# Retention followed by a SoLU feed-forward: chunk 3 loaded before w_out, w_out scaled mostly on GpSimd, key-value products moved next to the values, and new orders for the first chunks and the end

## The chip, the cores and the metric

The kernel runs on one core of a Trainium2 chip. The metric is the device time of one execution in microseconds (us). The kernel before takes 239.58 us, the median of 3 runs (239.53 to 240.38). One core has a matrix engine (TensorE, "PE" in the profile, with its weight loads as "PEld"), a vector engine (DVE), an activation engine (ACT), GpSimd (POOL) and a queue engine (SP) that here issues nearly all DMAs.

## The reference

Retention (causal attention with a decay per head and no softmax) over batch 8, heads 8, sequence 576, head size 64, and behind it a two-layer block with a SoLU activation and a layer norm, over all 4608 tokens:

```python
scores = q @ k.T / sqrt(64)                       # per batch and head
ret    = scores * where(i >= j, gamma[h] ** (i - j), 0)
x      = (ret @ v), heads side by side            # (4608, 512)
h      = x @ w_in                                 # (4608, 1024)
e      = exp(h - max(h))
solu   = h * e / sum(e)
ln     = (solu - mean(solu)) / sqrt(var(solu) + 1e-6) * g_ln
out    = ln @ w_out                               # (4608, 512)
```

All inputs and the output are float32; the kernel multiplies in float16.

## The kernel before

The tokens are cut into 36 chunks of 128 rows. Batches go in pairs: for one pair, chunks alternate between the two batches (four chunks of 128 positions each), and a ninth chunk takes the last 64 positions of both; that one is called a tail here. So chunks 8, 17, 26 and 35 are tails. Retention is computed in its chunked form: within a chunk by masked scores, and across chunks by a running state for each batch.

One chunk n goes through these helpers:

- `ld` (L111): three loads, q, k and v, of 256 KB each from SP's queue (six of half the size for a tail). Six chunks fit in the load pool.
- `cast` (L123): on GpSimd, q and v times the decay (two-input multiplies, L131 and L138), k cast to float16 (L137). For chunks 0 to 2 (`first`), q goes to DVE and k to ACT.
- `transpose_qk`, `evict_qk` (L149, L157): eight transposes on PE, and a copy out of PSUM by DVE or ACT.
- `scores`, `mask` (L168, L181): eight matmuls that use 64 rows of the array, and two masked copies on DVE.
- `state`, `state_update` (L192, L205, L208, L216): the key-value product `kp`, eight matmuls that write 64 columns of the array; DVE adds the old state, GpSimd decays it. Tails have neither.
- `values`, `evict_x` (L230, L236, L246): eight matmuls of 64 columns (masked scores times v), then four full-size ones (state times q), and a copy by ACT.
- `mm1`, `row_max`, `exps`, `solu` (L254, L263, L269, L279): x times w_in in eight matmuls of 512 columns; row maximum on DVE; exp on ACT; h times exp on DVE, with its sum.
- `spread` (L294 to L302): sum of squares on ACT, and three tiny GpSimd instructions that make the row scale `rs`.
- `transpose_u`, `evict_u` (L309, L314): eight transposes and a copy (ACT).
- `mm2`, `store` (L321, L328, L331): u times w_out in eight matmuls of 512 columns; ACT multiplies by `rs` on the way out; one DMA (two for a tail).

Before `mm2` can run for the first time, w_out is prepared once: `load_w_out` (four DMAs of 512 KB), `scale_w_out` (w_out times g_ln, cast to float16: eight ACT instructions, one for each block of 128 rows, L347), `mean_w_out` (L354, the column means by eight matmuls with a matrix of ones) and `centre_w_out` (L363, eight DVE instructions that write w_out anew with the means taken off, so that the layer norm's mean need not be taken from u).

The schedule is written by hand: each engine runs its instructions in the order of the program text, and an instruction waits for semaphores only. After a prologue (chunks 0 and 1 up to x, chunk 0 up to its exp), a loop over i runs from 1 to 36. Its turn i works on several chunks at once: transposes, scores, state and values of chunk i+1, the cast of chunk i+2, `mm1` of chunk i, `solu`, `spread` and `transpose_u` of chunk i-1, `evict_u` of chunk i-2, and `mm2` and `store` of chunk i-3 (LAG). In a turn, PE's order is: tp(i+1), h(i), sc(i+1), kp(i+1), o(i-3), x(i+1), lp(i-1), by the names of the tiles that are written. Turns 1 and 2 have another order (`early`): `mm1` and `row_max` come first, and the preparation of w_out stands in turn 2. The loads are issued in the order: chunks 0, 1, w_in, chunk 2, w_out, chunks 3, 4, 5; then one chunk in each turn. PSUM has four banks of a common tag `ps` (tp, sc, kp, o, x, lp, mean take turns in them) and two pairs of banks for h.

Of the kernel before, what the change touches and what calls it, by code (L numbers as in the profile page):

```python
# [10 lines left out]
FP = mybir.dt.float32  # L11
F16 = mybir.dt.float16
P = 128
H = 8
D = 64
LAG = 3
# [27 lines left out]
def kernel(  # L44
# [10 lines left out]
    nc = tc.nc  # L55
    B, _, S, _ = q.shape
    NTOK, DM = out.shape
    DFF = moe_w_in.shape[1]
    NF = DFF // P
    ACT = mybir.ActivationFunctionType  # L60
    ALU = mybir.AluOpType
# [23 lines left out]
    def rows(n):  # L85

        bs, c = chunks[n]
        if c < 4:
            return [(slice(0, P), bs[0], c * P)]
        return [(slice(64 * i, 64 * i + 64), b, 4 * P) for i, b in enumerate(bs)]  # L90
# [20 lines left out]
    def ld(n):  # L111
        qf = load.tile([P, H, D], FP, name="qf")
        kf = load.tile([P, H, D], FP, name="kf")
        vf = load.tile([P, H, D], FP, name="vf")
        for src, dst in ((q, qf), (k, kf), (v, vf)):
            for pp, b, s0 in rows(n):
                m = pp.stop - pp.start
                nc.sync.dma_start(  # L118
                    out=dst[pp], in_=src[b, :, s0 : s0 + m, :].rearrange("h p d -> p h d")
                )  # L120
        T["ld", n] = qf, kf, vf
# [32 lines left out]
    def evict_qk(n, copy=None):  # L154
        tp = T.pop(("tp", n))
        qkT = att.tile([P, 2, 4, P], F16, name="qkT")
        (copy or nc.vector.tensor_copy)(  # L157
            out=qkT.rearrange("p a b c -> p (a b c)"), in_=tp.rearrange("p a b c -> p (a b c)")
        )
        T["qkT", n] = qkT  # L160
# [88 lines left out]
    def mm1(n, by_rows=False):  # L249
        xT = T.pop(("xT", n))  # L250
        h = ps_h.tile([P, DFF], FP, name="h")
        order = [(i, dc) for i in range(2) for dc in range(4)]
        for i, dc in sorted(order, key=lambda o: o[1]) if by_rows else order:
            nc.tensor.matmul(  # L254
                out=h[:, i * 512 : (i + 1) * 512], lhsT=xT[:, dc],
                rhs=w_in16[:, dc, i * 512 : (i + 1) * 512],
                start=dc == 0, stop=dc == 3,
            )
        T["hps", n] = h

    def row_max(n):
        nm = tiny.tile([P, 1], FP, name="nm")
        nc.vector.tensor_reduce(out=nm, in_=T["hps", n], axis=AX.X, op=ALU.max, negate=True)  # L263
        T["nm", n] = nm

    def exps(n):
        e = moe.tile([P, DFF], FP, name="e")
        s = tiny.tile([P, 1], FP, name="s")
        nc.scalar.activation(  # L269
            out=e, in_=T["hps", n], func=ACT.Exp, bias=T.pop(("nm", n)), accum_out=s  # L270
        )
        T["e", n] = e, s

    def solu(n):
        e, s = T["e", n]
        u = moe.tile([P, DFF], F16, name="u")
        su = tiny.tile([P, 1], FP, name="su")
        nmu = tiny.tile([P, 1], FP, name="nmu")
        nc.vector.scalar_tensor_tensor(  # L279
            out=u, in0=T.pop(("hps", n)), scalar=1.0, in1=e, op0=ALU.mult, op1=ALU.mult,  # L280
            accum_out=su,
        )
        nc.vector.tensor_scalar(  # L283
            out=nmu, in0=su, scalar1=-1.0 / DFF, scalar2=None, op0=ALU.mult, op1=ALU.bypass
        )
        T["u", n] = u, nmu
# [16 lines left out]
        T["rs", n] = rs  # L303

    def transpose_u(n):
        u, _ = T.pop(("u", n))
        lp = ps.tile([P, NF, P], F16, tag="ps", name="lp")
        for c in range(NF):
            nc.tensor.transpose(out=lp[:, c], in_=u[:, c * P : (c + 1) * P], identity=ident)  # L309
        T["lp", n] = lp  # L310
# [3 lines left out]
        (copy or nc.scalar.copy)(out=uT, in_=T.pop(("lp", n)))  # L314
        T["uT", n] = uT

    def mm2(n):
        uT = T.pop(("uT", n))
        o = ps.tile([P, DM], FP, tag="ps", name="o")
        for c in range(NF):  # L320
            nc.tensor.matmul(  # L321
                out=o, lhsT=uT[:, c], rhs=w_out16[:, c], start=c == 0, stop=c == NF - 1
            )
        T["o", n] = o

    def store(n):
        o_sb = moe.tile([P, DM], FP, name="o_sb")
        nc.scalar.activation(out=o_sb, in_=T.pop(("o", n)), func=ACT.Copy, scale=T.pop(("rs", n)))  # L328
        for pp, b, s0 in rows(n):
            m = pp.stop - pp.start  # L330
            nc.sync.dma_start(out=out[b * S + s0 : b * S + s0 + m, :], in_=o_sb[pp])  # L331

    def load_w_in(a):
        nc.sync.dma_start(out=w_in32[:, a], in_=moe_w_in[a * P : (a + 1) * P, :])  # L334
# [7 lines left out]
        w = moe_w_out.rearrange("(c p) m -> p c m", p=P)  # L342
        nc.sync.dma_start(out=w_out32[:, 2 * i : 2 * i + 2], in_=w[:, 2 * i : 2 * i + 2])  # L343

    def scale_w_out(cs):
        for c in cs:
            nc.scalar.activation(  # L347
                out=w_out16[:, c], in_=w_out32[:, c], func=ACT.Copy, scale=g32[:, c : c + 1]
            )

    def mean_w_out():
        mean = ps.tile([P, DM], FP, tag="ps", name="mean")
        for c in range(NF):
            nc.tensor.matmul(  # L354
                out=mean, lhsT=ones, rhs=w_out16[:, c], start=c == 0, stop=c == NF - 1
            )
        T["mean"] = mean
# [10 lines left out]
    def on(j):  # L368
        return 0 <= j < NCH

    with tc.manual_schedule():
        nc.sync.dma_start(out=small, in_=nc.inline_tensor(small_np, name="small_c").ap())
        ld(0)
        nc.scalar.dma_start(out=ident, in_=nc.inline_tensor(id_np, name="ident_c").ap())
        nc.scalar.dma_start(
            out=tris.rearrange("p a b -> p (a b)"), in_=nc.inline_tensor(tris_np, name="tris_c").ap()
        )
        nc.scalar.dma_start(out=gln, in_=moe_g_ln.rearrange("(c p) -> p c", p=P))
        ld(1)
        for a in range(4):  # L380
            load_w_in(a)
        ld(2)
        for i in range(4):
            load_w_out(i)
        ld(3)
        ld(4)
        ld(5)
        nc.vector.memset(ones, 1.0 / DFF)
        nc.vector.memset(mhalf, -0.5)


        cast(0, True)
        nc.gpsimd.tensor_scalar(
            out=g32, in0=gln, scalar1=32.0, scalar2=None, op0=ALU.mult, op1=ALU.bypass
        )
        transpose_qk(0)
        evict_qk(0)
        scores(0)
        state(0)
        cast(1, True)  # L400
        transpose_qk(1)
        mask(0)
        state_update(0)
        values(0)
        evict_x(0)
        evict_qk(1)
        scores(1)
        state(1)
        mask(1)
        cast_w_in(0)  # L410
        cast_w_in(1)
        values(1)
        evict_x(1)
        cast_w_in(2)
        cast_w_in(3)
        state_update(1)
        mm1(0, True)
        row_max(0)
        cast(2, True)
        exps(0)  # L420

        for i in range(1, NCH + 1):
            if on(i + 5):
                ld(i + 5)
            early = i < 3
            if early:
                mm1(i)
                row_max(i)  # L430
            if i == 1:
                solu(0)
            if i == 2:
                solu(1)
                scale_w_out(range(NF))
                exps(2)
                mean_w_out()
            if on(i + 1):
                transpose_qk(i + 1)
                evict_qk(i + 1, nc.scalar.copy if i < 5 else None)  # L440
            if i == 1:
                exps(1)
            if on(i + 2):
                cast(i + 2)
            if not early:
                if on(i - 1):
                    solu(i - 1)
                if on(i):
                    mm1(i)
            if on(i - 2):  # L450
                evict_u(i - 2)
            if on(i + 1):
                scores(i + 1)
                mask(i + 1)
                if chunks[i + 1][1] < 4:
                    state(i + 1)
            if on(i - 1):
                spread(i - 1)
            if not early and on(i):
                row_max(i)  # L460
            if on(i + 1) and chunks[i + 1][1] < 4:
                state_update(i + 1)
            if i == 2:
                centre_w_out()
            if on(i - LAG):
                mm2(i - LAG)
                store(i - LAG)
            if i == NCH:
                for j in range(NCH - LAG + 1, NCH - 1):
                    mm2(j)  # L470
                    store(j)
            if on(i + 1):
                values(i + 1)
                evict_x(i + 1)
            if on(i - 1):
                transpose_u(i - 1)
            if not early and on(i):
                exps(i)
        evict_u(NCH - 1, nc.vector.tensor_copy)
        mm2(NCH - 1)  # L480
        store(NCH - 1)


# [28 lines left out]
```

## Time and profile before

| what | value |
|---|---|
| median of the runs | 239.58 us (239.53 to 240.38) |
| the profiled execution | 239.56 us, of which the span from first to last instruction is 237.8 us |
| mean granted TensorE clock | 0.992 |
| PE in the chain that ended last | 74% of the span |
| SP's queue in that chain | 12% |
| costliest PE groups | h (L254) 71.4 us, o (L321) 68.4 us |
| first matmul of h(4), the first turn of the loop's regular order that comes after w_out is ready | 44.42 us |
| first matmul of h(35), the last chunk | 221.30 us |

The span is what the profile's rows cover; 1.76 us of the execution lie around it. "Chain" is the chain of waits followed back from the last instruction. A group's row names the line, the engine, the tile written and the tiles read; chunk numbers in brackets are added here by counting, since the trace leaves buffer numbers out.

### The profile page before, as it was taken

How to read it: one execution, taken by the hardware profiler on the slowest of the kernel's cores; microseconds unless marked ns; L12 is line 12 of the kernel's file. 1: busy time of each engine (PE TensorE's matmuls, PEld its weight loads, DVE VectorE, ACT ScalarE, POOL GpSimd, SP SyncE). 2: the span in 40 equal slices, each digit the busy share in tenths (PEclk: the TensorE clock that was granted, in tenths of full speed). 3: DMA queues.
4: the chain of work that ended last, by engine and by line, in shares of the span. 5: the costliest groups of instructions: out<-in, count | busy, mean ns of one | idle time of the engine just before them, and what ended most of it. 6: DMA issues, size and time to landing. Idle time of an engine off the chain costs nothing.

```text
span 237.8 us, 5729 instructions
## 1 busy us (share of the span) xinstructions
PE 213.9 (90%) x2120; PEld 116.6 (49%) x2120; DVE 174.7 (73%) x294; ACT 172.7 (73%) x271; POOL 172.8 (73%) x275
## 2 busy tenths in 40 slices
PE   0586867899999999999999999999999999999971
PEld 0343334555555555555555555555555555555530
DVE  0537279878888888887788888888878888888530
ACT  2257994977787777777877777777777777777871
POOL 0275189898868899888869999998868999983220
PEclk9999799999999999999999999999999999999999
DMA  7999999998979694898788877978878876111123
GB/s 128 245 351 296 252 225 220 178 242 205 251 176 209 159 215 95 210 235 178 181 182 196 187 166 161 229 188 183 201 175 190 188 139 152 47 45 47 44 90 86
DMA packets 120923, 42.50 MB, mean 179 GB/s; under 512 B 114624, under 2 KB 114752, under 8 KB 120896
## 3 DMA queue, kind: packets, MB, share of 16 engines
q1 hardware_dynamic: 119568, 41.98, 76.5%
q10 hardware_dynamic: 1328, 0.17, 0.6%
q8 instruction: 16, 0.26, 0.5%
q14 instruction: 11, 0.09, 0.1%
HBM read 32.70 MB, written 9.44 MB: 177 GB/s over the span
## 4 chain that ended last, share of the span: by engine, by line
PE 74%; SPq 12%; DVE 4%; ACT 4%; DMA 2%; issue 2%; ACTq 0%
PE o L321 26%; PE h L254 22%; SPq L118 10%; PE tp L149 6%; PE lp L309 6%; PE x L230 5%; PE sc L168 4%; PE x L236 3%; PE kp L192 3%; DVE w_out L363 2%; DMA qf<-in_q_dram 2%; ACT e L269 1%; SPq L334 1%; DVE u L279 1%; SPq L343 1%
## 5 line engine op out<-in xcount | busy, mean ns | idle before, releaser
L254 PE MATMUL h<-w_in,xT 128*128 128x512 f16 x288 | 71.4, 392 | 0.8 <-ACT xT L246 0.5
L321 PE MATMUL o<-w_out,uT 128*128 128x512 f16 x288 | 68.4, 380 | 3.3 <-DVE w_out L363 1.5
L294 ACT ACTIVATE sq<-u,nmu 128x1024 f16<-128x1024 f16 x36 | 41.4, 1149 | 23.9 <-DVE nmu L283 23.9
L279 DVE SCALAR_TENSOR_TENSOR u<-h,e 128x1024 f16<-128x1024 f32 x36 | 44.1, 1224 | 10.9 <-ACT e L269 10.9
L263 DVE TENSOR_REDUCE nm<-h 128x1 f32<-128x1024 f32 x36 | 43.8, 1216 | 8.7 <-PE h L254 8.7
L181 DVE TENSOR_TENSOR ret<-sc,tris 128x512 f16<-128x512 f32 x72 | 46.1, 681 | 2.1 <-PE sc L168 2.1
L138 POOL TENSOR_TENSOR v<-vf,small 128x512 f16<-128x512 f32 x36 | 37.6, 1046 | 11.4 <-DMA vf<-in_v_dram 11.4
L208 POOL TENSOR_TENSOR s<-t,small 128x512 f16<-128x512 f32 x32 | 33.4, 1042 | 10.9 <-DVE t L205 8.4
L157 DVE COPY qkT<-tp 128x1024 f16<-128x1024 f16 x32 | 22.1, 692 | 25.5 <-PE tp L149 25.5
L321 PEld LDWEIGHTS <-uT 128*128 128x128 f16 x288 | 25.5, 98 | 31.3 <-issue 1.8
L254 PEld LDWEIGHTS <-xT 128*128 128x128 f16 x288 | 26.0, 100 | 30.0 <-issue 4.5
L269 ACT ACTIVATE e<-h,nm 128x1024 f32<-128x1024 f32 x36 | 40.3, 1120 | 0.0
L328 ACT ACTIVATE o_sb<-o,rs 128x512 f32<-128x512 f32 x36 | 24.6, 686 | 21.5 <-PE o L321 16.5
L131 POOL TENSOR_TENSOR q<-qf,small 128x512 f16<-128x512 f32 x33 | 34.4, 1042 | 6.8 <-DMA qf<-in_q_dram 6.8
L314 ACT COPY uT<-lp 128x1024 f16<-128x1024 f16 x35 | 35.5, 1015 | 0.0
L246 ACT CAST xT<-x 128x512 f16<-128x512 f32 x36 | 21.0, 584 | 2.6 <-PE x L236 1.3
L309 PE MATMUL lp<-ident,u 128*128 128x128 f16 x288 | 22.1, 219 | 0.0
L301 POOL TENSOR_TENSOR w<-w,ss 128x1 f32<-128x1 f32 x36 | 6.8, 189 | 20.8 <-ACT sq L294 18.9
L302 POOL TENSOR_TENSOR rs<-w,mhalf 128x1 f32<-128x1 f32 x36 | 19.8, 549 | 2.8
L149 PE MATMUL tp<-ident,q 128*128 128x128 f16 x144 | 14.3, 224 | 7.2 <-DVE q L131 6.7
L137 POOL CAST k<-kf 128x512 f16<-128x512 f32 x33 | 20.1, 610 | 0.0
L230 PE MATMUL x<-ret,v 128*64 128x128 f16 x288 | 16.2, 229 | 2.6 <-DVE ret L181 2.5
(37 smaller groups left out, 208.1 us busy)
## 6 DMA issues: line engine op xcount, KB each, us to landing
qf<-in_q_dram SPq DMA_DIRECT2D x32, 256.0 KB, 4.0
kf<-in_k_dram SPq DMA_DIRECT2D x32, 256.0 KB, 4.7
vf<-in_v_dram SPq DMA_DIRECT2D x32, 256.0 KB, 4.9
out_dram<-o_sb SPq DMA_DIRECT2D x32, 256.0 KB, 2.3
w_in<-in_moe_w_in_dram SPq DMA_DIRECT2D x4, 512.0 KB, 6.3
w_out<-in_moe_w_out_dram SPq DMA_DIRECT2D x4, 512.0 KB, 6.0
qf<-in_q_dram SPq DMA_DIRECT2D x8, 128.0 KB, 3.6
kf<-in_k_dram SPq DMA_DIRECT2D x8, 128.0 KB, 3.5
```

What stands on the lines that cost most here:

```text
L131: eq.tensor_tensor(out=q16, in0=qf, in1=a.unsqueeze(2).to_broadcast([P, H, D]), op=ALU.mult)
L138: nc.gpsimd.tensor_tensor(out=v16, in0=vf, in1=b.unsqueeze(2).to_broadcast([P, H, D]), op=ALU.mult)
L181: nc.vector.tensor_tensor(out=r, in0=sc[e], in1=m, op=ALU.mult)
L208: nc.gpsimd.tensor_tensor(out=s16, in0=t.unsqueeze(2).to_broadcast([P, 4, 2, D]), in1=gd.unsqueeze(3).to_broadcast([P, 4, 2, D]), op=ALU.mult,
L254: nc.tensor.matmul(out=h[:, i * 512 : (i + 1) * 512], lhsT=xT[:, dc], rhs=w_in16[:, dc, i * 512 : (i + 1) * 512], start=dc == 0, stop=dc == 3,
L263: nc.vector.tensor_reduce(out=nm, in_=T["hps", n], axis=AX.X, op=ALU.max, negate=True)
L269: nc.scalar.activation(out=e, in_=T["hps", n], func=ACT.Exp, bias=T.pop(("nm", n)), accum_out=s)
L279: nc.vector.scalar_tensor_tensor(out=u, in0=T.pop(("hps", n)), scalar=1.0, in1=e, op0=ALU.mult, op1=ALU.mult, accum_out=su,)
L294: nc.scalar.activation(out=sq, in_=u, func=ACT.Square, bias=nmu, accum_out=ss)
L309: nc.tensor.transpose(out=lp[:, c], in_=u[:, c * P : (c + 1) * P], identity=ident)
L314: (copy or nc.scalar.copy)(out=uT, in_=T.pop(("lp", n)))
L321: nc.tensor.matmul(out=o, lhsT=uT[:, c], rhs=w_out16[:, c], start=c == 0, stop=c == NF - 1)
```

## The change

`ld(3)` is issued ahead of the four loads of w_out instead of behind them. `scale_w_out` runs its first six blocks on GpSimd and the last two on ACT. Turns 1 to 3 are written out, with the preparation of w_out spread over turns 2 and 3. From turn 3 on, `state` and `state_update` stand behind `mm2` and `store`, directly ahead of `values`. `evict_qk` goes to ACT for chunks 2 and 4 of these turns, and to DVE for chunk 3 and all from 5 on. In the last turn, `exps(35)` stands directly behind `row_max(35)`, ahead of `store(32)`; behind the loop the order is new, the copy of `lp(34)` goes to DVE, `mm2(34)` stands behind `transpose_u(35)`, and the last `mm2` and `store` are cut in two halves of 256 columns.

```diff
-    def mm2(n):
+    def mm2(n, parts=1):
         uT = T.pop(("uT", n))
-        o = ps.tile([P, DM], FP, tag="ps", name="o")
-        for c in range(NF):
-            nc.tensor.matmul(
-                out=o, lhsT=uT[:, c], rhs=w_out16[:, c], start=c == 0, stop=c == NF - 1
-            )
-        T["o", n] = o
+        T["o", n] = []
+        w = DM // parts
+        for i in range(parts):
+            o = ps.tile([P, w], FP, tag="ps", name="o")
+            for c in range(NF):
+                nc.tensor.matmul(
+                    out=o, lhsT=uT[:, c], rhs=w_out16[:, c, i * w : (i + 1) * w],
+                    start=c == 0, stop=c == NF - 1,
+                )
+            T["o", n].append(o)
...
-    def scale_w_out(cs):
-        for c in cs:
-            nc.scalar.activation(
-                out=w_out16[:, c], in_=w_out32[:, c], func=ACT.Copy, scale=g32[:, c : c + 1]
-            )
+    def scale_w_out():
+        for c in range(NF):
+            if c < 6:
+                nc.gpsimd.tensor_scalar(
+                    out=w_out16[:, c], in0=w_out32[:, c], scalar1=g32[:, c : c + 1],
+                    scalar2=None, op0=ALU.mult, op1=ALU.bypass,
+                )
+            else:
+                nc.scalar.activation(
+                    out=w_out16[:, c], in_=w_out32[:, c], func=ACT.Copy, scale=g32[:, c : c + 1]
+                )
...
         ld(2)
+        ld(3)
         for i in range(4):
             load_w_out(i)
-        ld(3)
         ld(4)
         ld(5)
...
+        ld(6)
+        mm1(1)
+        row_max(1)
+        solu(0)
+        transpose_qk(2)
+        evict_qk(2, nc.scalar.copy)
+        exps(1)
+        cast(3)
+        scores(2)
+        mask(2)
+        state(2)
+        state_update(2)
+        spread(0)
+        values(2)
+        evict_x(2)
+        transpose_u(0)
+
+        ld(7)
+        transpose_qk(3)
+        evict_qk(3)
+        solu(1)
+        mm1(2)
+        evict_u(0)
+        scores(3)
+        mask(3)
+        spread(1)
+        scale_w_out()
+        row_max(2)
+        state(3)
+        state_update(3)
+        values(3)
+        evict_x(3)
+        transpose_u(1)
+        exps(2)
+
+        ld(8)
+        mean_w_out()
+        mm1(3)
+        cast(4)
+        solu(2)
+        centre_w_out()
+        transpose_qk(4)
+        evict_qk(4, nc.scalar.copy)
+        cast(5)
+        evict_u(1)
+        scores(4)
+        mask(4)
+        spread(2)
+        row_max(3)
+        mm2(0)
+        store(0)
+        state(4)
+        state_update(4)
+        values(4)
+        evict_x(4)
+        transpose_u(2)
+        exps(3)
+
+        for i in range(4, NCH):
             if on(i + 5):
                 ld(i + 5)
...
+            last = i == NCH - 1
+            if not last:
                 transpose_qk(i + 1)
-                evict_qk(i + 1, nc.scalar.copy if i < 5 else None)
+                evict_qk(i + 1)
             if on(i + 2):
                 cast(i + 2)
+            solu(i - 1)
+            mm1(i)
+            evict_u(i - 2)
+            if not last:
                 scores(i + 1)
                 mask(i + 1)
+                spread(i - 1)
+            row_max(i)
+            if last:
+                exps(i)
+            mm2(i - LAG)
+            store(i - LAG)
+            if not last:
                 if chunks[i + 1][1] < 4:
                     state(i + 1)
+                    state_update(i + 1)
                 values(i + 1)
                 evict_x(i + 1)
+            transpose_u(i - 1)
+            if not last:
                 exps(i)
+        n = NCH - 1
+        evict_u(n - 1, nc.vector.tensor_copy)
+        spread(n - 1)
+        solu(n)
+        mm2(n - 2)
+        store(n - 2)
+        transpose_u(n)
+        evict_u(n, nc.vector.tensor_copy)
+        spread(n)
+        mm2(n - 1)
+        store(n - 1)
+        mm2(n, 2)
+        store(n)
```

`store` loops over the parts of `o` in the same way and issues its DMAs for each part.

More of the change, by code (lines that the diff above doesn't have):

```diff
@@ L305, in transpose_u @@
     def transpose_u(n):
-        u, _ = T.pop(("u", n))
+        u, _ = T["u", n]
         lp = ps.tile([P, NF, P], F16, tag="ps", name="lp")
@@ L315, in evict_u @@
         T["uT", n] = uT
-    def mm2(n):
+    def mm2(n, parts=1):
         uT = T.pop(("uT", n))
-        o = ps.tile([P, DM], FP, tag="ps", name="o")
-        for c in range(NF):
-            nc.tensor.matmul(
-                out=o, lhsT=uT[:, c], rhs=w_out16[:, c], start=c == 0, stop=c == NF - 1
-            )
-        T["o", n] = o
-    def store(n):
[L327 to L331, printed above, removed]
+        T["o", n] = []
[8 more added lines that the diff above has]
+            T["o", n].append(o)
+    def store(n):
+        rs = T.pop(("rs", n))
+        os = T.pop(("o", n))
+        w = DM // len(os)
+        for i, o in enumerate(os):
+            o_sb = moe.tile([P, w], FP, tag=f"o_sb{w}", name="o_sb")
+            nc.scalar.activation(out=o_sb, in_=o, func=ACT.Copy, scale=rs)
+            for pp, b, s0 in rows(n):
+                m = pp.stop - pp.start
+                nc.sync.dma_start(
+                    out=out[b * S + s0 : b * S + s0 + m, i * w : (i + 1) * w], in_=o_sb[pp]
+                )
     def load_w_in(a):
@@ L343, in load_w_out @@
         nc.sync.dma_start(out=w_out32[:, 2 * i : 2 * i + 2], in_=w[:, 2 * i : 2 * i + 2])
-    def scale_w_out(cs):
-        for c in cs:
-            nc.scalar.activation(
-                out=w_out16[:, c], in_=w_out32[:, c], func=ACT.Copy, scale=g32[:, c : c + 1]
-            )
+    def scale_w_out():
[8 more added lines that the diff above has]
+                    out=w_out16[:, c], in_=w_out32[:, c], func=ACT.Copy, scale=g32[:, c : c + 1]
+                )
     def mean_w_out():
@@ L420 @@
         exps(0)
-        for i in range(1, NCH + 1):
+        ld(6)
[21 more added lines that the diff above has]
+        scores(3)
@@ L425 @@
+        store(0)
[6 more added lines that the diff above has]
+        for i in range(4, NCH):
             if on(i + 5):
                 ld(i + 5)
[L427 to L437, printed above, removed]
@@ L438 @@
-            if on(i + 1):
+            last = i == NCH - 1
+            if not last:
                 transpose_qk(i + 1)
-                evict_qk(i + 1, nc.scalar.copy if i < 5 else None)
-            if i == 1:
-                exps(1)
+                evict_qk(i + 1)
             if on(i + 2):
                 cast(i + 2)
[L445 to L451, printed above, removed]
@@ L452 @@
-            if on(i + 1):
+            solu(i - 1)
+            mm1(i)
+            evict_u(i - 2)
+            if not last:
                 scores(i + 1)
                 mask(i + 1)
+                spread(i - 1)
[5 more added lines that the diff above has]
+            if not last:
                 if chunks[i + 1][1] < 4:
                     state(i + 1)
-            if on(i - 1):
-                spread(i - 1)
@@ L459 @@
[L459 to L472, printed above, removed]
+                    state_update(i + 1)
@@ L473 @@
                 values(i + 1)
                 evict_x(i + 1)
-            if on(i - 1):
-                transpose_u(i - 1)
-            if not early and on(i):
+            transpose_u(i - 1)
+            if not last:
                 exps(i)
-        evict_u(NCH - 1, nc.vector.tensor_copy)
-        mm2(NCH - 1)
-        store(NCH - 1)
+        n = NCH - 1
[5 more added lines that the diff above has]
+        transpose_u(n)
```

## The prediction

> **What bounds the kernel now.** I read the page's shares first, then PE in steady turns, then the first 45 us engine by engine, then the end. PE is busy 90% of the span and holds 74% of the chain:
>
> ```profile
> PE 213.9 (90%) x2120; PEld 116.6 (49%) x2120; DVE 174.7 (73%) x294; ACT 172.7 (73%) x271; POOL 172.8 (73%) x275
> PEclk9999799999999999999999999999999999999999
> ```
>
> A steady turn on PE (timeline; start, busy time):
>
> ```profile
> 204.40 1.90 PE L254 MATMUL h<-w_in,xT 128*128 128x512 f16 x8
> 206.23 0.40 PE L168 MATMUL sc<-qkT 64*128 64x128 f16 x8
> 206.56 0.32 PE L192 MATMUL kp<-v,k 128*64 128x64 f16 x8
> 206.81 1.90 PE L321 MATMUL o<-w_out,uT 128*128 128x512 f16 x8
> 208.63 0.41 PE L230 MATMUL x<-ret,v 128*64 128x128 f16 x8
> 208.98 0.40 PE L236 MATMUL x<-qkT,s 128*128 128x128 f16 x4
> 209.22 0.61 PE L309 MATMUL lp<-ident,u 128*128 128x128 f16 x8
> 209.66 0.39 PE L149 MATMUL tp<-ident,q 128*128 128x128 f16 x4
> ```
>
> Nothing waits: h(i) to h(i+1) is 210.11 - 204.40 = 5.71 us, and the turn is one row of groups. But the starts hide a price. Starts within h are (1.90 - 0.39) / 7 = 0.216 apart (0.39 is one matmul), so eight take 1.73; the next group starts after 1.83. Where the tile shape (the "128*64" column) stays the same there is no such gap: eight lp starts at 0.056 make 0.45, and tp follows after 0.44. So changing the shape costs about 0.1: h to sc 0.10, sc to kp 0.33 - 4 pairs x 0.052 = 0.12, kp to o 0.25 - 4 x 0.028 = 0.14, o to x 0.10, x to its second group 0.35 - 0.21 = 0.14. Five changes, 0.60 us a turn.
>
> Up to h(4) at 44.42 PE isn't the bound. DVE, in the timeline:
>
> ```profile
> 24.66 0.42 DVE L205 TENSOR_TENSOR t<-kp,s 128x256 f32<-128x256 f32 x1
> 29.59 1.22 DVE L263 TENSOR_REDUCE nm<-h 128x1 f32<-128x1024 f32 x1 [4.51 <-PE h L254]
> 35.05 5.35 DVE L363 SCALAR_TENSOR_TENSOR w_out<-w_out,g,mean 128x512 f16<-128x512 f32 x8
> 40.32 1.22 DVE L279 SCALAR_TENSOR_TENSOR u<-h,e 128x1024 f16<-128x1024 f32 x1
> ```
>
> The eight centrings end at 40.40, and o(0) starts at 40.45: it waits for all of them. DVE idles 4.51 us ahead of them, for h(2), which runs slowly: the windows view (busy us and counts of PE, PEld, DVE, ACT, POOL; clock; DMA share; GB/s) shows the next fact:
>
> ```profile
> 22.36:25.77 3.41, 1.82 (x36) 1.44 (x36) 2.69 (x6) 2.91 (x6) 0.00 (x0) 1.00 1.06 371
> 25.77:29.18 3.41, 3.24 (x12) 1.05 (x10) 0.00 (x0) 3.41 (x7) 0.43 (x1) 0.50 0.84 178
> ```
>
> After a window with 1.82 us of PE work the next one is granted half the clock. POOL stands still in the first of them: chunk 3's q lands at 28.7.
>
> The end, from the timeline:
>
> ```profile
> 225.69 1.11 ACT L269 ACTIVATE e<-h,nm 128x1024 f32<-128x1024 f32 x1
> 226.92 1.23 DVE L279 SCALAR_TENSOR_TENSOR u<-h,e 128x1024 f16<-128x1024 f32 x1 [1.98 <-ACT e L269]
> 230.23 0.69 DVE L314 COPY uT<-lp 128x1024 f16<-128x1024 f16 x1 [1.89 <-PE lp L309]
> 230.98 1.90 PE L321 MATMUL o<-w_out,uT 128*128 128x512 f16 x8 [0.79 <-DVE uT L314]
> 233.05 0.69 ACT L328 ACTIVATE o_sb<-o,rs 128x512 f32<-128x512 f32 x1 [2.22 <-PE o L321]
> 233.77 1.16 SPq L331 DMA_DIRECT2D out_dram<-o_sb  x2
> ```
>
> From e(35) on it is a chain of latencies; the first DMA of the last store is issued at 233.77, 4.03 us before the span ends.
>
> **Part 1: kp next to x.** PE's turn becomes tp, h, sc, o, kp, x, lp. kp and x have the same shape, so one change of five goes. Shape by shape: 0.10 + 0.12 + 0.10 + 0.02 (kp's slower first pair stays) + 0.14 = 0.48, which saves 0.12 us. It holds in turns 4 to 34 but for those with a tail as chunk i+1 (8, 17, 26, 35): 31 - 4 = 27 turns, 3.2 us. sc to o is a change that the trace lacks; bounds are the cheapest and dearest changes, 0.10 and 0.14, I take 0.12; the ends move the total by 0.5. Does another engine bind at 5.59 us? DVE's work per turn is 5.0 (0.69 + 1.45 + 1.28 + 1.22 + 0.42), ACT's 4.9, POOL's 5.31 by the distances of its starts, with 0.40 idle waiting for t. kp now ends some 4.9 us after tp starts, and DVE takes t at 5.1 anyway, behind `row_max`: that queue covers the delay. If the cover were gone, every 0.1 would delay s (POOL) by 0.1, which is needed two chunks later. o moves up 0.24 and needs uT, done 0.3 earlier. The PSUM bank that tp takes frees with o_sb, earlier than before. I book nothing for these.
>
> **Part 2: the head.** Up to lp(0) at 25.35 nothing of DVE, ACT or PE moves (same data, same order); at SP, chunk 3's three loads pass four loads of w_out. 256-byte loads land 1.2 us apart, so q, k and v of chunk 3 land near 22.0, 23.2 and 24.4 instead of 28.7 to 30.7, and w_out's last piece at 27.9 + 3.6 = 31.5 instead of 27.9; chunk 4 follows at its old time, since the bytes ahead of it are the same.
> POOL: cast(3) ends at 25.5, state_update(2) (1.04 + 0.61) at 27.1, spread(0) at 28.2. Then spread(1) blocks the scaling behind it: PE does lp(0), tp(3) at half clock to 26.8, DVE copies tp (0.69) and makes u(1) to 28.9, ACT's sq(1) lasts to 30.4, and POOL is free at 31.3.
> The six scalings: no row shows a GpSimd tensor_scalar of this size. The nearest are a one-input cast (0.61) and two-input multiplies (1.04) of 128x512:
>
> ```profile
> L138 POOL TENSOR_TENSOR v<-vf,small 128x512 f16<-128x512 f32 x36 | 37.6, 1046 | 11.4 <-DMA vf<-in_v_dram 11.4
> L137 POOL CAST k<-kf 128x512 f16<-128x512 f32 x33 | 20.1, 610 | 0.0
> L298 POOL TENSOR_SCALAR w<-s 128x1 f32<-128x1 f32 x36 | 9.5, 264 | 3.3 <-ACT e L269 3.3
> ```
>
> It reads one tensor, so I take the cast plus the 0.06 by which a small tensor_scalar is dearer than a small two-input instruction (0.26 against 0.19): 0.67, starts 0.62 apart. Six end at 35.0; the upper end, 1.04, gives 37.3. Behind them on POOL queue state_update(3) and cast(4); tp(4) waits for the latter until 38.3, which the centring covers.
> The Trainium skill, "GPSIMD Engine Reference", section "3.1 Elementwise — side-by-side cycle accounting", speaks against the move: about 2.6 cycles an element at 1.2 GHz, an estimated 1.1 us each, and its advice is DVE for elementwise work. By that the sum below would rise by some 2.3 us; the cast's row (0.61) contradicts it for one input, and the two-input rows (1.04) agree.
> Meanwhile h(2) runs 26.8 to 29.75 (half clock to 29.18), sc(3), mask(3) to 31.5, nm(2) to 32.7; ACT scales the last two blocks from 31.5 to 32.8, xT(3) to 33.5, e(2) to 34.6; DVE u(2) with nmu to 36.05. PE: mean ends at 35.7. So centring runs 36.05 to 41.35 (before: 35.05 to 40.40), but u(2), which stood behind it, is now done. Then o(0) 41.4 to 43.2, kp(4), x(4), lp(2), tp(5), and h(4) at 44.85, against 44.42: 0.43 later. If o followed centring block by block it would be 44.1; the trace's o(0) waited for all. Turn 4 gives 0.5 back: before, h(4) to h(5) took 6.22 us, since ACT made qkT (1.01) ahead of uT; now DVE does. Net 0.07 earlier.
>
> **Part 3: the end.** h(35) keeps its distance to the turns before. e(35) follows nm directly: 0.64 earlier (225.05). u(35) ends at 227.5, lp 228.05, uT 228.95, while o(34) fills PE to 229.75. ACT's order is o_sb(32), sq(34), o_sb(33), sq(35) to 229.95, then o_sb(34); rs(35) is ready at 230.9. The halves of o(35) end at 230.8 and 231.7 (256 columns: 0.11 a matmul, half of 0.216; eight weight loads more of 0.098 fit under it). A half's o_sb costs 0.47 (0.69 less 256 elements at 0.84 ns, from 0.58 for 512 and 1.01 for 1024); first half 231.0 to 231.5. Its two DMAs hold SP (0.51 + 0.59) to 232.6, past the second half's o_sb (232.2), so the last pair issues at 232.65 instead of 233.77: 1.1 us saved. Bounds: 0, if rs(35) or SP is late, and 1.6, if SP doesn't hold it.
>
> **Sum.** 239.56 - 0.07 - 3.2 - 1.1 = 235.2 us, against the profiled execution (span 237.8 and 1.76 around it), which is 0.02 off the median.
>
> **Rivals.** (A) A scaling costs 1.04: six starts 0.38 further apart, 2.3 us, less 0.3 that DVE's u(2) covers: 237.2. For it: every POOL row but the casts; against: one input. (B) Moving kp saves nothing, the change doesn't do what it says: kp's slow start or a bank's wait eats the 0.12. 235.2 + 3.2 = 238.4. Against: no gap in all three same-shape joins. (C) Slower: GpSimd's scaling alone turns the head into a loss. From 0.72 us on, each 0.1 of a scaling delays mean, centring, o(0) and all 32 turns behind by 0.6; from 0.72 + 4.4 / 6 = 1.45 us it outweighs all gains, and at 2.1, double the dearest row of that size, the time is 243.5. For it: POOL's pow takes 0.55 for one element, so its price depends on the operation; against: no 128x512 row is over 1.05.
>
> **How the numbers follow.** Forecast 0.60, A 0.15, B 0.11, C 0.14. 235.2 is the likeliest; its own range is 233.5 (o block by block 0.75, end 0.5, part 1 0.5) to 236.3 (the end saves nothing). The range goes on over A towards B: 233.3 to 238.3; C and the rest of B stay out. 0.5% is 1.2 us, about what a measurement of this kernel tells from no change: forecast and A are faster, B (-0.5%) counts half as same; of C a little is same. Faster 0.80, same 0.07, slower 0.13.
>
> **What would show it.** Right: 5.59 us from h to h with kp between o and x; six POOL rows near 0.67 from 31.3 on; centring at 36; h(4) near 44.9; e(35) ahead of o_sb(32). Wrong: PE idle before kp, x or tp in steady turns; scalings of 1 us and more; w_out's last piece later than 31.5, behind which ACT holds back xT(3), e(2) and the centring one for one.

## The result and the profile after

The changed kernel takes 240.6 us (median of 6 runs, 240.06 to 240.97); the kernel before, in 6 runs, takes 239.41 us. The ratio is 1.0048, with a 95% interval of 1.0025 to 1.0071: slower by half a per cent, where 235.2 us and a gain were forecast.

The profiled execution of the changed kernel took 240.06 us, of which the span is 238.25 (237.78 before). Its page, engine shares and granted clock:

```profile
PE 213.0 (89%) x2128; PEld 116.5 (49%) x2128; DVE 177.1 (74%) x297; ACT 168.4 (71%) x263; POOL 182.4 (77%) x281
...
PEclk9999785799999999999999999999999999999997
```

The shares look as before, and POOL is 10 us busier. Where the time went is seen by cutting both spans at the first matmul of h(4) and of h(35):

| stage | before | after | difference |
|---|---|---|---|
| start to h(4) (the head) | 44.42 | 50.71 | +6.3 |
| h(4) to h(35) | 176.88 | 172.60 | -4.3 |
| h(35) to the end | 16.48 | 14.94 | -1.5 |

Two stages gained 5.8 us, more than the 4.8 that were forecast, and the head gave it all back and 0.5 more. The middle stage first: a steady turn on PE after the change (timeline; start, busy time):

```profile
206.58 1.90 PE L254 MATMUL h<-w_in,xT 128*128 128x512 f16 x8
208.41 0.40 PE L168 MATMUL sc<-qkT 64*128 64x128 f16 x8
208.74 1.90 PE L325 MATMUL o<-w_out,uT 128*128 128x512 f16 x8
210.57 0.32 PE L192 MATMUL kp<-v,k 128*64 128x64 f16 x8
210.72 0.39 PE L230 MATMUL x<-ret,v 128*64 128x128 f16 x8
211.05 0.40 PE L236 MATMUL x<-qkT,s 128*128 128x128 f16 x4
```

kp now takes 0.15 us from its start to that of x, instead of 0.25 to that of o. The next h starts at 212.18: 5.60 us a turn instead of 5.71.

The head. The GpSimd group of the scalings by form (mean ns of one behind the comma), and then its rows and DVE's in the timeline:

```profile
L359 POOL TENSOR_SCALAR w_out<-w_out,g 128x512 f16<-128x512 f32 x6 | 9.3, 1566 | 0.0
```

```profile
30.34 9.29 POOL L359 TENSOR_SCALAR w_out<-w_out,g 128x512 f16<-128x512 f32 x6
...
39.60 1.04 POOL L208 TENSOR_TENSOR s<-t,small 128x512 f16<-128x512 f32 x1
...
40.91 3.62 PE L254 MATMUL h<-w_in,xT 128*128 128x512 f16 x8
...
41.23 5.36 DVE L380 SCALAR_TENSOR_TENSOR w_out<-w_out,g,mean 128x512 f16<-128x512 f32 x8 [6.08 <-POOL s L216]
...
50.71 1.89 PE L254 MATMUL h<-w_in,xT 128*128 128x512 f16 x8
```

One scaling takes 1.57 us. The six run back to back from 30.34 to 39.6; the column means need them, and centring starts at 41.23 instead of 35.05, after DVE has idled 6.08 us. The last row shown is the start of h(4). (The row of the centring blames a GpSimd instruction that ended at that moment; what centring reads is the mean, whose last matmuls ran from 39.68 to 41.1.) The windows view shows what the wait did to the clock (busy us and counts of PE, PEld, DVE, ACT, POOL; clock; DMA share; GB/s):

```profile
30.98:34.39 3.41, 1.23 (x11) 0.55 (x9) 1.38 (x3) 2.72 (x5) 3.41 (x3) 1.00 0.90 203
34.39:37.80 3.41, 1.17 (x2) 0.21 (x2) 0.73 (x3) 0.00 (x0) 3.41 (x3) 0.50 1.24 223
37.80:41.20 3.40, 2.10 (x5) 0.66 (x5) 0.00 (x0) 0.00 (x0) 3.40 (x5) 0.50 1.33 219
41.20:44.60 3.40, 3.40 (x11) 1.34 (x10) 3.37 (x6) 0.00 (x0) 3.40 (x5) 0.50 1.33 210
```

PE gets one matmul for each scaling, every 1.5 us; three windows in a row are granted half the clock, and h(3) at 40.91 takes 3.62 us instead of 1.89.

### The profile page after: what moved, and what is told of

The parts are those of the page before. It is cut to its first block, busy times and chain, and to the rows that moved or that the text cites. A ratio compares the mean times of both kernels' runs of the same rounds, so it can differ in the third digit from the quotient of the medians.

```text
span 238.2 us, 5743 instructions
## 1 busy us (share of the span) xinstructions
PE 213.0 (89%) x2128; PEld 116.5 (49%) x2128; DVE 177.1 (74%) x297; ACT 168.4 (71%) x263; POOL 182.4 (77%) x281
## 4 chain that ended last, share of the span: by engine, by line
PE 80%; DVE 5%; ACT 3%; issue 3%; POOL 3%; DMA 2%; SPq 2%; ACTq 0%; POOLq 0%
PE o L325 26%; PE h L254 25%; PE tp L149 7%; PE lp L309 7%; PE sc L168 5%; PE x L230 3%; PE x L236 3%; PE kp L192 3%; POOL w_out L359 2%; DMA kf<-in_k_dram 2%; DVE u L279 2%; SPq L118 2%; DVE nm L263 1%; DVE ret L181 1%; ACT e L269 1%
## 5 line engine op out<-in xcount | busy, mean ns | idle before, releaser
L325 PE MATMUL o<-w_out,uT 128*128 128x512 f16 (+1 forms) x296 | 68.2, 374 | 0.5 <-ACT uT L314 0.5
L279 DVE SCALAR_TENSOR_TENSOR u<-h,e 128x1024 f16<-128x1024 f32 x36 | 44.1, 1224 | 10.1 <-ACT e L269 9.7
L157 DVE COPY qkT<-tp 128x1024 f16<-128x1024 f16 x34 | 23.5, 692 | 24.7 <-PE tp L149 24.7
L254 PEld LDWEIGHTS <-xT 128*128 128x128 f16 x288 | 26.6, 101 | 30.1 <-issue 5.0
L325 PEld LDWEIGHTS <-uT 128*128 128x128 f16 x296 | 26.3, 98 | 29.3 <-issue 0.5
L337 ACT ACTIVATE o_sb<-o,rs 128x512 f32<-128x512 f32 (+1 forms) x37 | 25.0, 675 | 14.2 <-POOL w L298 4.7
L314 ACT COPY uT<-lp 128x1024 f16<-128x1024 f16 x34 | 34.5, 1014 | 0.3 <-PE lp L309 0.3
L309 PEld LDWEIGHTS <-u 128*128 128x128 f16 x288 | 17.6, 99 | 1.9 <-DVE u L279 0.9
```

The source lines that it names most:

```text
L254: nc.tensor.matmul(out=h[:, i * 512 : (i + 1) * 512], lhsT=xT[:, dc], rhs=w_in16[:, dc, i * 512 : (i + 1) * 512], start=dc == 0, stop=dc == 3,
L279: nc.vector.scalar_tensor_tensor(out=u, in0=T.pop(("hps", n)), scalar=1.0, in1=e, op0=ALU.mult, op1=ALU.mult, accum_out=su,)
L325: nc.tensor.matmul(out=o, lhsT=uT[:, c], rhs=w_out16[:, c, i * w : (i + 1) * w], start=c == 0, stop=c == NF - 1,)
```

## The experiments

All times are medians of four to ten runs beside runs of the kernel before (medians 239.2 to 239.6 us), but for two that were run once, which are named so; starts are read from one profiled execution each. Two theories stood against each other: the price of a GpSimd scaling sets the head (1), or the new order of turns 1 to 3 is dear whoever scales (2).

### Who scales: ACT, or GpSimd by a two-input multiply

```diff
 act_scale
-            if c < 6:
+            if c < 0:
                 nc.gpsimd.tensor_scalar(
 two_input_scale
-                nc.gpsimd.tensor_scalar(
-                    out=w_out16[:, c], in0=w_out32[:, c], scalar1=g32[:, c : c + 1],
-                    scalar2=None, op0=ALU.mult, op1=ALU.bypass,
-                )
+                nc.gpsimd.tensor_tensor(
+                    out=w_out16[:, c], in0=w_out32[:, c],
+                    in1=g32[:, c : c + 1].to_broadcast([P, DM]), op=ALU.mult,
+                )
```

> All eight scalings of w_out on ACT, in the place where the changed kernel has them; everything else as changed. Theory 1 (the price of a GpSimd scaling, 1.57 us in the changed kernel's trace, sets the head): ACT is free at 29.4 and scales to 34.4, xT(3), e(2) and u(2) follow to 37.5, centring to 43.0, so h(4) comes near 46.5 instead of 50.7, and the time is 236.4 us (235.5 to 237.5). Theory 2 (the new order of turns 1 to 3 is dear whoever scales, through the later w_out and the half clock): h(4) stays near 50 and the time at 239.5 to 240.6.

Measured: 234.99 us, ratio 0.9834 (0.9792 to 0.9876), 0.5 under the expected range. h(4) starts at 45.51, centring at 37.45. DVE's wait in the head is now one for ACT, which scales first and makes e(2) after it:

```profile
36.09 1.22 DVE L279 SCALAR_TENSOR_TENSOR u<-h,e 128x1024 f16<-128x1024 f32 x1 [4.99 <-ACT e L269]
...
37.45 5.36 DVE L380 SCALAR_TENSOR_TENSOR w_out<-w_out,g,mean 128x512 f16<-128x512 f32 x8
```

> The six GpSimd scalings as two-input multiplies with g broadcast along the row, the form that takes 1.04 us in every trace so far. Theory 1: six starts 0.54 closer together, the sixth ends 3.2 us earlier, centring starts near 38.0 instead of 41.2, and the time falls by 3.2 to 237.4 us (236.5 to 238.4). Theory 2: the head stays where it is, 239.8 to 240.6.

Measured: 237.18 us, ratio 0.9898 (0.9861 to 0.9935); the six take 1.04 us each, centring starts at 38.10, h(4) at 46.75. (The six runs fall into two of 235.6 and 236.1 and four of 237.1 to 237.5; the starts are those of the one that took 236.07.) Theory 1 holds in both: centring starts 3.8 and 3.1 us sooner than in the changed kernel, as expected, and the time falls by 5.6 and 3.4. Two runs with one edit each move the start of centring and the time together; nothing of the order was touched.

### The old head, and the other parts one by one

`old_head` keeps the changed loop from turn 4 on and the changed end; turns 1 to 3, the order of the loads and the scaling are as before. `kp_only` and `end_only` are the kernel before with one part of the change each:

```diff
 kp_only
                 if on(i + 1):
                     scores(i + 1)
                     mask(i + 1)
-                    if chunks[i + 1][1] < 4:
+                    if i < 3 and chunks[i + 1][1] < 4:
                         state(i + 1)
...
+            if i >= 3 and on(i + 1) and chunks[i + 1][1] < 4:
+                state(i + 1)
+                state_update(i + 1)
             if on(i + 1):
                 values(i + 1)
```

> Turns 1 to 3, the order of the loads and the scaling (eight on ACT) as before; the loop from turn 4 on and the end as changed. Both theories: the head is back (h(4) near 44.4), the steady turns keep 5.60 us and the end its 14.9 us behind h(35), so 239.4 - 3.0 (27 turns x 0.11) - 0.5 (turn 4 without its wait on ACT) - 1.6 = 234.3 us (233.8 to 235.3). If the shorter turn or end needs the new head, it stays over 236.

Measured: 233.66 us, ratio 0.976 (0.9728 to 0.9792), 0.6 under the sum and 0.1 under the expected range. (In its profiled execution, 234.32 us, h(4) starts at 45.08 and not at 44.4; `end_only`, the old head once more, has 44.87. The old head alone varies by 0.7 us between executions.) So the shorter turn and end need nothing of the new head.

> The kernel before with one edit: from turn 3 on, state and state_update stand behind store, directly ahead of values. If a change of the array's tile shape costs about 0.1 us: 27 turns go from 5.71 to 5.60 us, with turn 3's own 28, and the time is 239.2 - 3.1 = 236.1 us (235.6 to 236.7). If the shorter turn needs the new head, or the gain came from elsewhere: 239 and turns of 5.71.

Measured: 235.92 us, ratio 0.9841 (0.9814 to 0.9867). h(4) to h(35) takes 172.79 us (windows view), close to the 172.60 of the changed kernel; the end takes 16.5, as before:

```profile
44.46:217.25 172.79, 172.23 (x1816) 95.01 (x1813) 144.78 (x243) 139.99 (x219) 148.05 (x231) 1.00 0.77 175
```

The move alone is worth 3.7 us.

> The kernel before with the new end alone (exps(35) ahead of store(32), the order behind the loop, the last mm2 and store in halves). From the changed kernel's trace the span ends 14.9 us behind h(35) instead of 16.5, so 239.2 - 1.5 = 237.7 us (237.1 to 238.3). The prediction's own term was 1.1, which would give 238.1.

Measured: 237.95 us, ratio 0.9942 (0.9919 to 0.9965). The middle stage is 176.88 us, as before, and the end 14.94.

The parts add up: 3.7 + 1.7 = 5.4 us, and `old_head`, which has both, is 5.5 under the kernel before.

### What makes the GpSimd instruction dear

```diff
 fixed_number_scale
-                    out=w_out16[:, c], in0=w_out32[:, c], scalar1=g32[:, c : c + 1],
+                    out=w_out16[:, c], in0=w_out32[:, c], scalar1=32.0,
 forms (one form for each of the first six blocks)
+            elif c == 2:
+                nc.gpsimd.tensor_scalar(
+                    out=w_out16[:, c], in0=w_out32[:, c], scalar1=32.0,
+                    scalar2=1.0, op0=ALU.mult, op1=ALU.mult,
+                )
...
+            elif c == 4:
+                nc.gpsimd.tensor_copy(out=w_out16[:, c], in_=w_out32[:, c])
```

> The six GpSimd scalings multiply by a fixed number instead of by g_ln, so g_ln is left out of six of the eight blocks. It measures what makes the instruction dear. If it is the operand with one number per row: 0.6 to 0.7 us each, and the time is near 235.5. If it is the tensor_scalar instruction as such: 1.57 us each and 240.6.

Measured: 1.49 us each, and 240.28 us in a single run. The operand with one number per row is not what costs.

> One look at what a GpSimd instruction of 128x512 costs by its form, each of the first six blocks in another: tensor_scalar with one number per row; the same in two halves of 256; tensor_scalar with two fixed numbers and two multiplies (leaves out g_ln); two-input multiply; plain copy (leaves out g_ln); and one block on DVE. If the price is per element: the halves 0.85 to 0.9 each, the full one 1.57. If the unused second operation is what costs, the form with two multiplies is no dearer than the one with one. Two-input 1.04, copy 0.61. The time itself is between 235 and 237.5.

Measured, in a single run of 235.75 us, in GpSimd's timeline (block 0; block 1 in halves; blocks 2, 3, 4):

```profile
30.55 1.82 POOL L359 TENSOR_SCALAR w_out<-w_out,g 128x512 f16<-128x512 f32 x1
32.36 1.82 POOL L366 TENSOR_SCALAR w_out<-w_out,g 128x256 f16<-128x256 f32 x2
34.15 0.62 POOL L371 TENSOR_SCALAR w_out<-w_out 128x512 f16<-128x512 f32 x1
34.73 1.04 POOL L376 TENSOR_TENSOR w_out<-w_out,g 128x512 f16<-128x512 f32 x1
35.72 0.61 POOL L381 CAST w_out<-w_out 128x512 f16<-128x512 f32 x1
```

Two halves cost what one whole block does: the price is per element, with hardly a fixed part. The form with two real multiplies takes 0.62, a third of the form whose second operation is bypassed. (That form took 1.82 here and 1.57 in the changed kernel; why these two differ stays open.)

That leaves one operand to change:

```diff
 two_multiplies
                 nc.gpsimd.tensor_scalar(
                     out=w_out16[:, c], in0=w_out32[:, c], scalar1=g32[:, c : c + 1],
-                    scalar2=None, op0=ALU.mult, op1=ALU.bypass,
+                    scalar2=1.0, op0=ALU.mult, op1=ALU.mult,
                 )
```

> The changed kernel with one operand and one operation of its six GpSimd scalings replaced: a second multiply by 1.0 where the second operation was bypassed; the result is the same. Theory 1 with the empty second operation as the cause: 0.6 to 0.7 us each instead of 1.57, the sixth ends near 34.0, centring starts near 35.2, and the time is what the prediction's sum gave for 0.67, 235.2 us, or up to 1 us less, since act_scale and old_head came out 0.6 to 1.4 under their sums (234.0 to 235.6). If the operand with one number per row is what costs: 1.5 us each and 240.6.

Measured: 233.08 us, ratio 0.9742 (0.9708 to 0.9776), 0.9 under the expected range. The group and the head:

```profile
L359 POOL TENSOR_SCALAR w_out<-w_out,g 128x512 f16<-128x512 f32 x6 | 4.0, 693 | 0.0
```

```profile
30.90 4.03 POOL L359 TENSOR_SCALAR w_out<-w_out,g 128x512 f16<-128x512 f32 x6
...
35.89 5.36 DVE L380 SCALAR_TENSOR_TENSOR w_out<-w_out,g,mean 128x512 f16<-128x512 f32 x8 [0.55 <-DMA kf<-in_k_dram]
...
40.52 1.89 PE L325 MATMUL o<-w_out,uT 128*128 128x512 f16 x8 [0.51 <-ACT uT L314]
...
44.13 1.89 PE L254 MATMUL h<-w_in,xT 128*128 128x512 f16 x8
```

A second multiply by one, which computes nothing, takes the changed kernel from 0.5% slower to 2.6% faster. Order, engines and loads are untouched, so the form of that second operation is the cause of the loss. The edit changes its operand and its operation together (a fixed number and a multiply for none and a bypass); which of the two the price hangs on was not told apart.

### Other splits, and the order of the loads

`dve_act_scale` gives four blocks to DVE (0.48 us each) and four to ACT; `four_and_four` gives four to GpSimd in the two-multiply form and four to ACT; `four_late_load` is the latter with chunk 3 loaded behind w_out:

```diff
 four_late_load, beside four_and_four
         ld(2)
-        ld(3)
         for i in range(4):
             load_w_out(i)
+        ld(3)
```

> The changed kernel with the six GpSimd scalings split up: four on DVE, four on ACT. Theory 1: ACT is done with scaling at 32.0, since the last piece of w_out lands at 30.7; e(2) runs to 33.7 and u(2) to 35.2, so centring ends at 40.6 instead of 42.8 with eight on ACT; 235.0 - 2.2 = 232.8 us (232.0 to 234.0), under both the kernel before and every variant so far. If a DVE scaling from SBUF is as dear as a GpSimd one, the four take 6 us and the time is over 236.

Measured: 233.28 us, ratio 0.9741 (0.9713 to 0.9769).

> The same with four blocks on GpSimd and four on ACT. The last block is then set by ACT (w_out's last piece lands at 30.7, so 32.0) and not by GpSimd; mean is done at 32.8, mm1(3) and tp(4) come 1.5 us sooner, but centring still waits for u(2) at 35.2. Theory 1: the same as two_multiplies within 0.7 us, or up to 1 us less if fewer windows fall to half the clock. 233.0 to 235.0.

Measured: 232.92 us, ratio 0.9722 (0.9699 to 0.9746), the fastest by its median, though its interval overlaps those of `two_multiplies`, `dve_act_scale` and `old_head`. It is 0.1 under its expected range. Against `old_head` at 233.66 the new head, with its scaling mended, is thus worth 0.7 us at best, which these intervals don't separate.

> The same as four_and_four, but chunk 3 loaded behind w_out as in the kernel before. Chunk 3's q lands 6 us later, so tp(3), which now stands ahead of solu(1) and mm1(2) on PE and DVE, waits for GpSimd's cast to 30.4 instead of starting at 25.6: the head is longer by 3 to 5 us, 236.5 to 239.5. If the order of the loads does not matter: within 0.5 of four_and_four.

Measured: 237.24 us, ratio 0.9904 (0.9882 to 0.9926): the later load costs 4.3 us in this order. PE stands for the cast of chunk 3:

```profile
28.55 1.04 POOL L131 TENSOR_TENSOR q<-qf,small 128x512 f16<-128x512 f32 x1 [7.07 <-DMA qf<-in_q_dram]
...
29.65 0.61 PE L149 MATMUL tp<-ident,q 128*128 128x128 f16 x4 [3.31 <-POOL q L131]
```

So the early load belongs to the new head. Whether it would help the old head, which asks for chunk 3 later, was not tried.

## Why the prediction was wrong, by its own steps

**The step that failed is the term for the scalings**: "I take the cast plus the 0.06 by which a small tensor_scalar is dearer", 0.67 us, with 1.04 as the upper end. Measured: 1.57, outside both. The bounds were taken from rows of the same shape and engine, one-input and two-input, but none of them had a second operation that is bypassed, and that is what costs. L298, the small tensor_scalar that gave the 0.06 (its rows give 0.07), has two multiplies; with two multiplies the scaling takes 0.69, so the guess was right for the form it was taken from. The one bypassed GpSimd row of the trace before is L393, and eight numbers a row are too few to show a price per element:

```profile
L393 POOL TENSOR_SCALAR g<-gln 128x8 f32<-128x8 f32 x1 | 0.2, 244 | 0.0
```

A row of another operation bounds nothing when the price hangs on the operation; the text said so itself about pow in rival C, and drew no wider bound from it.

**Rival C came true, by its own formula.** It put the head's price at 6 us for each us of a scaling over 0.72, and the turning point at 1.45: 235.2 + 6 x (1.57 - 0.72) = 240.3, against 240.06 in the profiled execution. That it meets so closely is partly luck: the formula puts h(4) at 44.85 + 5.1 = 49.95, 0.8 sooner than measured, and the other two stages gained 1.0 more than forecast. It had a chance of 0.14. The range, built on the bound of 1.04, left it out.

**Part 1 was right in mechanism and somewhat small.** The turn is 5.60 us, forecast 5.59; sc to o is again 0.33 us from start to start, so that change costs the 0.12 that was taken for it. No other engine became the bound. The middle stage gained 4.3 us, forecast 3.2 + 0.5: counted from h(i) to h(i+1), five turns gained 0.23 to 0.25 instead of 0.12 each, and a sixth, turn 26, 0.51. They are those two behind each tail but the last, whose chunk i+1 has no older state. Against that, turns 15, 24 and 33 gained only 0.05, and turn 16 lost 0.24, which it doesn't in `kp_only`. Behind h(8), before the change, tp starts 0.64 us after lp instead of 0.45, just as DVE is done with t at 72.71:

```profile
72.13 0.62 PE L309 MATMUL lp<-ident,u 128*128 128x128 f16 x8
72.77 0.38 PE L149 MATMUL tp<-ident,q 128*128 128x128 f16 x4
```

With kp behind o it starts after 0.51 (77.44 to 77.95 in the changed kernel). That tp waited for kp's PSUM bank fits these times, but is argued only.

**Part 2, the rest of the head, was right within 1 us**: chunk 3 lands at 21.5, 22.7 and 23.8 (22.0, 23.2, 24.4), w_out's last piece at 30.7 (31.5), GpSimd is free at 30.3 (31.3). With the scalings at 0.69 centring starts at 35.89 (36.05) and h(4) at 44.13 (44.85, or 44.1 if o follows centring block by block). In that run o(0) runs in one piece at 40.52, ahead of the last block's end at 41.25, so it did not wait for all blocks as it did before, and the second of the two figures for h(4) is the one that came true. The forecast read the old trace's wait as one for all of w_out. `kp_only` speaks against that: with kp(4) and its update behind o(0) and nothing else moved in the head, o(0) starts 0.5 us before the last centring ends:

```profile
35.09 5.35 DVE L363 SCALAR_TENSOR_TENSOR w_out<-w_out,g,mean 128x512 f16<-128x512 f32 x8
...
39.90 1.90 PE L321 MATMUL o<-w_out,uT 128*128 128x512 f16 x8
```

In the old order the two tiles of sc(4), kp(4) and mean hold all four banks of `ps` until the last centring has read mean, so o(0) may have waited for a bank; that fits the times, but is argued only.

In the changed kernel h(4) lost 5.9 us against the forecast while centring lost 5.2. Most of the rest goes with the half clock, which the text had not priced. The chain of waits of the changed kernel (start, length, what) shows it:

```profile
39.68 1.44 PE mean L371 x3
41.12 3.41 PE h L254 x8
44.53 0.57 PE tp L149 x8
45.12 1.01 ACT qkT L157
46.14 0.92 ACT uT L314
47.10 1.89 PE o L325 x8
```

The slow h(3) holds up tp(4), behind it on ACT come qkT(4) and uT(1), and o(0) starts at 47.10, 0.5 us after centring is done. Centring isn't on this chain at all. Beside `two_multiplies`, where the same h(3) runs at the full clock in 1.89 us, centring starts 5.3 us later and h(4) 6.6 us; the 1.2 between them is of the size of h(3)'s 1.7 us more. No run has the long wait and the full clock, so this split is not shown by a single edit.

**Part 3 was right and small**: the last pair of DMAs is issued 1.15 us sooner behind h(35), forecast 1.1. From the issue of that pair to its last landing it is 2.65 us instead of 2.91, which makes 1.4 of the 1.5 that the end gained.

Rival A was the right kind, with too low a price: `two_input_scale` shows what 1.04 gives, 237.18 measured and 237.2 forecast. That agreement is luck in part too, since the other stages gained 1.0 more than the forecast had; its profiled execution took 236.07. Rival B fell: kp's move saved all that was forecast and more. In `two_multiplies`, where the scaling costs what was forecast, the three stages change by -0.3, -4.3 and -1.5, to 233.44 in the profiled execution. So with the failed term right, the forecast of 235.2 would still have been 1.8 too high: 0.7 at h(4), as o(0) didn't wait for all blocks, 0.6 in the middle and 0.4 at the end.

## What to carry to other kernels

Before an instruction moves to another engine, time that very form on it: operation by operation and slot by slot, not shape by shape. A new form multiplied by six and placed in a stage where nothing covers it decides the sign of a change, however solid the other terms are; where no row shows it, its bound has to be drawn as wide as the oddest row of that engine suggests. And it pays to put matmuls of the same tile shape next to each other: moving one group saved 3.7 us here, some 3.0 of it by the shorter turn (27 turns, 0.11 each).

## What the runs showed of the hardware that was not expected

- GpSimd's tensor_scalar on 128x512 (float32 to float16): 0.69 us with two multiplies and one number per row, 0.62 with two fixed numbers, but 1.49 to 1.82 with the second operation bypassed. A plain copy takes 0.61, a two-input multiply 1.04. DVE takes 0.48 for the bypassed form.
- The half clock doesn't need a long idle gap: windows of 3.41 us with 1.23 and 1.17 us of PE work, one matmul every 1.5 us, were followed by half speed. What separates the windows of these traces is the work in them: over the first 60 us of all thirteen, every window at full clock with up to 1.74 us of PE work was followed by half the clock, every one with 1.98 or more by the full one, and from 1.79 to 1.91 both occur. The Trainium skill, "TensorE: Matmul & The Clock Gate", section "Why this matters for your kernels", asks for no idle gaps over about 3 us between bursts; here the longest gaps in those two windows were 1.2 us, and the clock fell all the same.
